# Half of the last weight's quarters prepared in layer 3 and parked as split parts, and raw operands loaded ahead of the weight blocks

## The chip, the cores and the metric

The kernel runs on one core of a Trainium2 chip. A core has five engines that work side by side, each through its own queue of instructions in a fixed order: TensorE (PE, matmuls), VectorE (DVE), ScalarE (ACT), GpSimd (POOL) and SyncE (SP, which here only issues DMAs). DMAs are also issued from POOL's queue and, a few, from ACT's. The metric is the device time of one execution in microseconds; lower is better.

## The reference, cut to what matters

```python
proj = einsum('bhsd,df->bhsf', x, w_phi)           # for q and for k
proj = proj - max(abs(proj), axis=-1, keepdims=True)
phi  = concatenate([exp(proj), exp(-proj)], axis=-1)
kv   = einsum('bhsf,bhsd->bhfd', phi(k), v);  z = sum(phi(k), axis=2)
attn = einsum('bhsf,bhfd->bhsd', phi(q), kv) / (phi(q) . z + 1e-6)
x = attn reshaped to (2304, 512)
h = maximum(maximum(x @ w1, x @ w2), x @ w3)        # 512 -> 768, layer 1
x = h @ w_out                                       # 768 -> 512, layer 2
h = x @ w_in                                        # 512 -> 2048, layer 3
g = maximum(h, 0) + alpha * minimum(h, 0)
out = g @ w_out2                                    # 2048 -> 512, the output blocks
```

4 batches, 8 heads, 576 positions, so 2304 tokens. The weights arrive as 64-bit floats; the results must be good to float32.

## The kernel before, in words

**Accuracy.** Every operand of a large product is kept as two tiles, `hi` (the value rounded to TensorE's format, a copy by ACT, L70) and `lo` (the rest, a subtraction by VectorE, L76). A product is three matmuls: hi x hi, hi x lo, lo x hi. A weight comes in as raw 64-bit words (tile `st`, 512 KB, loaded at L496 by SP) and is turned into 32-bit floats (tile `wt`) by one ACT instruction (L83) and four of VectorE (L85 to L91). What is then added or subtracted between such tiles goes through `both` (L517).

**Stages.** The 16 attention pairs run first, interleaved with layer 1 (TensorE line L270, matmuls `p<-x,w123t`). Each result `ho` of layer 1 goes to DRAM (`h_d`, POOL, L446). Layer 2 (L664, matmuls `p<-x,wo`) has 8 steps `c`; it leaves sums of token halves in DRAM (`y_d`). Layer 3 (L757) works by a Strassen-Winograd scheme of seven products instead of eight: 16 units, unit n being token group `tp` = n // 4 and quarter `q` = n % 4 of the columns. A unit has three PSUM tiles, `pb`, `pc` and `sums`; `sums` is added to in steps and copied out by ACT between them (`kept`, tile `s`, L766), and one more copy goes into `g` (L806). TensorE may go on into `sums` only when the copy is done. The result goes through `prelu` (ACT `neg`, L776; VectorE, L777) and by POOL to DRAM (`g_d`, L778).

**The output blocks** (L841, matmuls `acc<-wq,o`) are 9 blocks of 256 tokens. Each takes the 2048 inputs in two halves, and a half is 7 products of 12 matmuls, 84 in all. For a half, `left` loads raw data `a` from `g_d` (L705, two DMAs of 512 KB), forms sums `wt` of them (L718 to L731) and splits seven operands `o`. The weights `wq` are 28 granules (`needs`, L735): 7 combinations of each of four pieces p of `w_out2`; p = 0, 1 serve half 0, p = 2, 3 half 1. The combinations are formed early (`do_quarters`, L532) and parked in DRAM as plain floats (`q_d`, L530, POOL). `split_q` (L737) later reads each back (L742, SP) and splits it on ACT and VectorE into a tile of the pool `ring` or `ring2`. Part of half 0 of block 0 is done between the matmuls of the last two units of layer 3; for block 0 the weights of half 0 are split in layer 3's last units, those of half 1 around its end.

**Order.** The functions that prepare weights put their steps in one list `todo`, in the order of L589: the four pieces of `w_out2`, then `w_out`, then the four quads of `w_in`. `convert(n)` takes n steps from its front: two per unit of layer 1, three per step of layer 2 (L683), three per unit of layer 3 (L811, where the list is soon empty). `stage` (L493) keeps loads of `st` ahead of their use, three at first. Tiles of one tag rotate through a fixed number of buffers, so a load waits until the old tile's last reader is done, and a tile placed in a closed pool's memory waits for the old pool's last users (the second half's `a` and the `o` of the output blocks take over memory that layer 3 used). A scheduler in the framework, which goes by dependencies, a cost model and priorities, then writes each engine's order; on the chip each engine keeps to it.

Of the kernel before, what the change touches and what calls it, by code (L numbers as in the profile page):

```python
# [19 lines left out]
P = 128  # L20
# [33 lines left out]
def tile_kernel(ctx: ExitStack, tc: tile.TileContext, qT, kT, tails, v, w_phi, w1, w2, w3, w_out, w_in, w_out2, alpha, out):  # L54
# [54 lines left out]
    r_d = dram.tile([B, NPAIR, 2, S], F32, name="r_d")  # L109
    g_d = dram.tile([NF2, P, NTOK], F32, name="g_d")  # L110
    y_d = dram.tile([NT2, 7, P, 2 * CH], F32, name="y_d")
    q_d = dram.tile([4, 7, P, 512], F32, name="q_d")

    def bank(tag, bufs, nm):
        return ps.tile([P, 512], F32, tag=tag, bufs=bufs, name=nm)
# [370 lines left out]
    def granule(pool, nm):  # L486

        return pool.tile([P, 2, 512], F32R, tag="w", name=nm)

    sources, staged = [], []  # L490
    todo = []

    def stage():  # L493
        if sources:
            st = big(U32, [P, 1024], "st")
            nc.sync.dma_start(st, sources.pop(0).bitcast(U32))  # L496
            staged.append(st)

    def big(dtype, shape, nm):
        return sp.tile(shape, dtype, tag="st", bufs=3, name=nm)  # L500

    def word():
        return sp.tile([P, 512], F32, tag="wt", bufs=8, name="wt")

    def words():

        wt = word()
        run(from_f64(staged.pop(0), wt))
        stage()
        return wt  # L510

    def split(dst, src):
        hi_act(dst[:, 0], src)
        sub(V, dst[:, 1], src, dst[:, 0])

    def both(dst, x, y, op=ALU.subtract):
        V.tensor_tensor(dst, x, y, op=op)  # L517
        return dst
# [7 lines left out]
    def do_out():  # L526
        return [lambda k=k: split_out(k) for k in range(NF1)], [w_out[k] for k in range(NF1)]

    def park(p, i, x):
        nc.gpsimd.dma_start(q_d[p, i], x)  # L530

    def do_quarters(p):  # L532
        b = {}

        def get(q):
            b[q] = words()

        def one():
            get(0)
            b[4] = both(word(), b[1], b[0])  # L540
            park(p, 0, b[0])
            park(p, 4, b[4])

        def two():
            get(3)
            park(p, 2, b[3])
            b[5] = both(word(), b[3], b[4])
            park(p, 5, b[5])
            park(p, 6, both(b[1], b[3], b[1]))

        def three_():
            get(2)
            park(p, 1, b[2])
            park(p, 3, both(word(), b[5], b[2]))

        return [lambda: get(1), one, two, three_], [w_out2[p, q] for q in (1, 0, 3, 2)]

    def do_quad(q):
        x = {}
        wi[q] = {}  # L560

        def get(n):
            x[n] = words()

        def to(i, n):
            pool = ring2 if (q == 0 and i < 4) or (q == 3 and i > 0) else ring
            wi[q][i] = granule(pool, "wi")
            split(wi[q][i], x[n])

        def second():  # L570
            get("22")
            x["s1"] = both(word(), x["21"], x["22"], ALU.add)

        def third():
            get("11")
            x["s2"] = both(word(), x["s1"], x["11"])
            x["s3"] = both(x["21"], x["11"], x["21"])
            to(0, "11")

        def fourth():  # L580
            get("12")
            to(1, "12")
            x["s4"] = both(x["12"], x["12"], x["s2"])

        steps = [lambda: get("21"), second, third, fourth]
        steps += [lambda i=i, n=n: to(i, n) for i, n in zip(range(2, 7), ("s2", "s1", "s3", "22", "s4"))]
        return steps, [w_in[q, a, b] for a, b in ((1, 0), (1, 1), (0, 0), (0, 1))]

    for steps, src in [do_quarters(p) for p in range(4)] + [do_out()] + [do_quad(q) for q in range(4)]:  # L589
        todo += steps  # L590
        sources += src

# [19 lines left out]
    def convert(n):  # L612
        for _ in range(min(n, len(todo))):
            todo.pop(0)()
# [38 lines left out]
    for c in range(2 * B):  # L653
        p2 = [double(tag, "p2") for tag in SETS[c % 2]]
        if c == 0:
            p2.reverse()
        if c + 1 < 2 * B:
            for kk in range(NF1 // 2):
                load_h(c + 1, kk)
        for ms in ((0, 1), (2, 3)) if c == 0 else (range(KT),):  # L660
            for k, m in ((k, m) for k in range(NF1) for m in ms):
                cs = slice(m * P, (m + 1) * P)
                for n, (x, y) in enumerate(three(wo[k][:, 0, cs], wo[k][:, 1, cs], *hs[c, k])):
                    nc.tensor.matmul(p2[m // 2][1][:, m % 2], x, y, start=k + n == 0, stop=k == NF1 - 1 and n == 2)  # L664
        tp = c // 2
        for b in range(2):
            Y[b, c % 2] = yo = z_tile("yo")
            A.activation(yo, p2[b][1], AF.Copy)
            if c % 2 == 0:
                nc.scalar.dma_start(y_d[tp, b], flat(yo))  # L670
        if c % 2:
            nc.scalar.dma_start(y_d[tp, 6], flat(Y[1, 1]))
            t1, t2, t3 = (z_tile("yt") for _ in range(3))
            both(t1, Y[0, 1], Y[0, 0])
            both(t2, Y[1, 1], t1)
            both(t3, Y[1, 1], Y[0, 1])
            t4 = both(Y[1, 0], Y[1, 0], t2)
            for i, t in zip((2, 3, 4, 5), (t2, t1, t3, t4)):
                nc.gpsimd.dma_start(y_d[tp, i], flat(t))
        if c == 2 * B - 1:  # L680
            for i in range(6):
                load_y(0, i)
        convert(3)  # L683

    T = P
    ORDER = (0, 5, 6, 4, 1, 3, 2)
# [5 lines left out]
            return (None, ring2, ring2, ring2, ring2, ring, ring)[n]  # L692
        return None if half == 0 and n == 0 else op4

    def left(block, half):

        ready[block, half] = res = {}
        if half and block:
            a = up.tile([P, 2, 4, 2 * T], F32, tag="a", bufs=1, name="a")
            a = [a[:, kh] for kh in range(2)]  # L700
        else:
            a = [big(F32, [P, 4, 2 * T], "a") for _ in range(2)]
        for kh in range(2):
            r = slice(kh * 8 + half * 4, kh * 8 + half * 4 + 4)
            nc.sync.dma_start(a[kh], g_d[r, :, block * 2 * T : (block + 1) * 2 * T].rearrange("f p n -> p f n"))  # L705
        (a00, a10), (a01, a11) = ((x[:, :, :T], x[:, :, T:]) for x in a)
        s1, s2, s3, s4 = (word().rearrange("p (f n) -> p f n", f=4) for _ in range(4))

        def factor(i, src):
            home = factor_home(block, half, len(res))  # L710
            o = granule(home, "o") if home else big(F32R, [P, 2, 512], "o")
            ov = o.rearrange("p a (f n) -> p a f n", f=4)
            hi_act(ov[:, 0], src)
            sub(V, ov[:, 1], src, ov[:, 0])
            res[i] = o

        factor(0, a00)
        V.tensor_tensor(s1, a10, a11, op=ALU.add)  # L718
        V.tensor_tensor(s2, s1, a00, op=ALU.subtract)
        yield  # L720
        factor(5, s2)
        V.tensor_tensor(s3, a00, a10, op=ALU.subtract)
        yield
        factor(6, s3)
        yield
        factor(4, s1)
        yield
        factor(1, a01)
        yield
        factor(3, a11)  # L730
        V.tensor_tensor(s4, a01, s2, op=ALU.subtract)  # L731
        yield
        factor(2, s4)
# [3 lines left out]
    def split_q(count):  # L737
        for _ in range(count):
            n = len(wq)
            p, i = needs[n]  # L740
            wl = word()
            nc.sync.dma_start(wl, q_d[p, i])  # L742
            wq[p, i] = granule(ring if n < 16 or n >= 26 else ring2, "wq")
            split(wq[p, i], wl)

    load_y(0, 6)

# [40 lines left out]
    for n, (tp, q) in enumerate(units):  # L788
        sums, u1 = nxt
        if (tp, q) == (NT2 - 1, 0):  # L790
            convert(len(todo))
        g0, g1 = result(), result()
        _, pb = double("db", "pb")
        mults(pb, tp, q, 1, True)
        V.tensor_tensor(g0[:, :, 0], pb, u1, op=ALU.add)
        mults(sums, tp, q, 2, False)
        u2 = kept(sums)
        _, pc = double("dc", "pc")
        mults(pc, tp, q, 3, True)
        mults(sums, tp, q, 4, False)  # L800
        u3 = kept(sums)
        V.tensor_tensor(g1[:, :, 1], pc, u3, op=ALU.add)
        if n + 1 < len(units):
            nxt = begin(n + 1)
        mults(sums, tp, q, 5, False)
        A.activation(g1[:, :, 0], sums, AF.Copy)  # L806
        mults(pc, tp, q, 6, False)
        V.tensor_tensor(g0[:, :, 1], pc, u2, op=ALU.add)  # L808
        prelu(g1, tp, 4 * q + 2)
        prelu(g0, tp, 4 * q)  # L810
        convert(3)  # L811
        if tp == NT2 - 1:
            if q == 0:
                first = left(0, 0)
                run(first)
            split_q((2, 7, 7, 7)[q])
    zp_ctx.close()
    xp_ctx.close()
# [103 lines left out]
```

## Time and profile before

| | |
|---|---|
| median of 3 runs | 886.14 us (883.64 to 888.54) |
| profiled execution | 882.21 us, span 880.4 us |
| TensorE busy | 869.1 us (99%) |
| VectorE busy | 678.7 us (77%) |
| ACT busy | 490.8 us (56%) |
| POOL busy | 158.3 us (18%) |
| mean granted TensorE clock | 0.998 |

A row of a timeline reads: start, duration, engine, line, operation, out<-in, size, how many of the same in a row, and in brackets how long the engine had been idle and what ended that. Matmuls overlap in the pipeline, so the distance of starts, and not the duration of one, is their pace. The granted clock is a share of the full 2.4 GHz.

### The profile page before, as it was taken

Reading aid. Unit: us, or ns where it says so; the run is one execution under the profiler, and the core shown is the slowest. Engines: PE = TensorE matmul, PEld = TensorE weight load, DVE = VectorE, ACT = ScalarE, POOL = GpSimd, SP = SyncE. Lnnn points to the kernel's source line nnn. Section 1 sums busy time; section 2 is a strip of 40 time slices with the busy share of each in tenths; the row PEclk is TensorE's granted clock in tenths of the full one; section 3 lists DMA queues with packets and bytes.
Section 4 is the critical chain, followed back from the end, with each engine's and each line's share of the span. In section 5 each row is a group of like instructions: output and inputs, shape, how many; then the busy total and the mean of one; then the engine's idle time right before and its main releaser. Section 6 shows DMA issues by size and latency. Waiting matters only on the chain.

```text
span 880.4 us, 17440 instructions
## 1 busy us (share of the span) xinstructions
PE 869.1 (99%) x6631; PEld 856.2 (97%) x6631; DVE 678.7 (77%) x1290; ACT 490.8 (56%) x1017; POOL 158.3 (18%) x278
## 2 busy tenths in 40 slices
PE   9999999999999999999999999999999999999998
PEld 8888999999999999999999999999999999999998
DVE  5689878778887879889999454746488889977791
ACT  4677657677776752334365354646477654444440
POOL 0354213222232135331101001111111100000000
PEclk9999999999999999999999999999999999999999
DMA  6455553222332158886489644835358645544321
GB/s 233 140 159 168 169 180 91 77 79 89 85 90 76 29 176 286 291 276 191 159 284 304 203 147 146 271 131 194 111 183 267 214 152 173 165 123 140 120 73 48
DMA packets 70436, 142.99 MB, mean 162 GB/s; under 512 B 9152, under 2 KB 36176, under 8 KB 70352
## 3 DMA queue, kind: packets, MB, share of 16 engines
q1 hardware_dynamic: 53664, 92.95, 33.8%
q0 software_dynamic: 14816, 45.26, 15.0%
q10 hardware_dynamic: 1872, 3.67, 1.2%
q8 instruction: 52, 0.85, 0.4%
q14 instruction: 32, 0.26, 0.1%
HBM read 93.07 MB, written 46.34 MB: 158 GB/s over the span
## 4 chain that ended last, share of the span: by engine, by line
PE 85%; DVE 6%; DMA 4%; issue 2%; ACT 1%; POOL 1%; DVEq 0%; POOLq 0%; ACTq 0%; SPq 0%
PE acc L841 20%; PE p L270 17%; PE sums L757 11%; PE p L664 8%; PE pj L270 6%; PE pn L270 6%; PE pc L757 6%; PE kvp L298 3%; PE kvp L311 3%; PE pb L757 3%; PE pt L373 2%; DVE wt L89 1%; DVE wt L91 1%; DMA xr<-h_d 1%; DMA nd<-nd 1%
## 5 line engine op out<-in xcount | busy, mean ns | idle before, releaser
L270 PE MATMUL p<-x,w123t 128*128 128x288 f32 x1728 | 249.1, 298 | 0.9 <-DVE ho L444 0.9
L270 PEld LDWEIGHTS p<-x,w123t 128*128 128x128 f32 x1728 | 234.5, 188 | 2.2 <-DVE ho L444 1.1
L841 PE MATMUL acc<-wq,o 128*128 128x256 f32 x1512 | 182.3, 283 | 2.5 <-ACT o L70 2.2
L841 PEld LDWEIGHTS acc<-wq,o 128*128 128x128 f32 x1512 | 181.5, 190 | 2.9 <-ACT o L70 2.4
L757 PE MATMUL sums<-x,wi 128*128 128x288 f32 x768 | 107.7, 295 | 0.3 <-ACT s L766 0.3
L757 PEld LDWEIGHTS sums<-x,wi 128*128 128x128 f32 x768 | 103.9, 188 | 0.6 <-ACT s L766 0.6
L664 PE MATMUL p<-x,wo 128*128 128x288 f32 x576 | 77.1, 296 | 1.5 <-ACT x L70 0.8
L664 PEld LDWEIGHTS p<-x,wo 128*128 128x128 f32 x576 | 76.6, 188 | 1.9 <-ACT x L70 1.0
L70 ACT ACTIVATE o<-wt 128x512 fp32r<-128x512 f32 x72 | 44.4, 629 | 56.4 <-PE acc L841 28.6
L777 DVE SCALAR_TENSOR_TENSOR g<-neg,al,g 128x576 f32<-128x576 f32 x64 | 50.1, 811 | 23.7 <-ACT neg L776 23.7
L217 DVE TENSOR_REDUCE mx<-pj 128x4 f32<-128x512 f32 (+1 forms) x80 | 49.7, 629 | 18.4 <-PE pj L270 18.1
L766 ACT ACTIVATE s<-sums 128x576 f32<-128x576 f32 x48 | 31.1, 648 | 45.4 <-PE sums L757 44.1
L778 POOL DMA_DIRECT2D g_d<-g x32 | 22.9, 714 | 162.5 <-DVE g L777 160.2
L446 POOL DMA_DIRECT2D h_d<-ho x48 | 27.8, 579 | 120.5 <-DVE ho L444 102.6
L76 DVE TENSOR_TENSOR o<-wt,o 128x512 fp32r<-128x512 f32 x72 | 48.0, 681 | 1.7 <-ACT o L70 1.7
L83 ACT ACTIVATE wt<-st 128x512 f32<-128x512 f32 x38 | 25.3, 673 | 41.7 <-DMA st<-in_w_out 33.4
L250 ACT ACTIVATE ke<-pj,mx 128x128 f32<-128x128 f32 x96 | 36.5, 380 | 20.1 <-DVE mx L217 20.1
L70 ACT ACTIVATE o<-a 128x512 fp32r<-128x512 f32 x54 | 33.1, 626 | 19.8 <-PE acc L841 18.5
L776 ACT ACTIVATE neg<-g 128x576 f32<-128x576 f32 x64 | 40.1, 675 | 6.2 <-DVE g L808 5.9
L251 ACT ACTIVATE ke<-pj,my 128x128 f32<-128x128 f32 x96 | 37.0, 386 | 11.0 <-DVE my L248 10.8
L298 PEld LDWEIGHTS kvp<-v,ke 128*128 128x128 f32 x320 | 40.1, 191 | 2.1 <-ACT ke L243 0.3
L298 PE MATMUL kvp<-v,ke 128*128 128x128 f32 x320 | 41.8, 276 | 0.0
(155 smaller groups left out, 1699.5 us busy)
## 6 DMA issues: line engine op xcount, KB each, us to landing
g_d<-g POOLq DMA_DIRECT2D x32, 576.0 KB, 3.6
a<-g_d SPq DMA_DIRECT2D x36, 512.0 KB, 4.4
st<-in_w_out SPq DMA_DIRECT2D x22, 512.0 KB, 5.3
wst<-in_w SPq DMA_DIRECT2D x18, 512.0 KB, 4.8
st<-in_w_in SPq DMA_DIRECT2D x16, 512.0 KB, 3.8
yr<-y_d SPq DMA_DIRECT2D x28, 288.0 KB, 3.4
v<-in_v SPq DMA_DIRECT2D x16, 480.0 KB, 3.6
q_d<-wt POOLq DMA_DIRECT2D x28, 256.0 KB, 6.0
```

The costliest lines, as they stand in the source:

```text
L70: A.activation(dst, src, AF.Copy)
L76: eng.tensor_tensor(dst, src, hi.bitcast(F32), op=ALU.subtract)
L217: V.tensor_reduce(mx, pv, axis=AX.X, op=ALU.max, apply_absolute_value=True, negate=True)
L250: A.activation(ev[:, a, 0], pv[:, a], AF.Exp, bias=mx[:, a : a + 1])
L251: A.activation(ev[:, a, 1], pv[:, a], AF.Exp, bias=my[:, a : a + 1], scale=-1.0)
L270: nc.tensor.matmul(dst, x, y, start=i == 0, stop=i == len(ops) - 1, **kw)
L298: nc.tensor.matmul(kvp[:, j * P : (j + 1) * P], e[:, c], rv[:, t, j // 2 : j // 2 + 2].rearrange("p a d -> p (a d)"), start=first, stop=t ...
L664: nc.tensor.matmul(p2[m // 2][1][:, m % 2], x, y, start=k + n == 0, stop=k == NF1 - 1 and n == 2)
L757: nc.tensor.matmul(dst[:, j], a, b, start=start and n == 0, stop=n == len(ops) - 1, skip_group_check=True)
L776: A.activation(neg, gv[:, j], AF.Relu, scale=-1.0)
L777: V.scalar_tensor_tensor(gv[:, j], neg, al[:, f + j : f + j + 1], gv[:, j], op0=ALU.mult, op1=ALU.add)
L841: nc.tensor.matmul(acc[i], x, y, start=half == 0 and f == 0 and n == 0 and place[i][1] == 0, stop=half == 1 and f == 3 and n == 2, skip_gr ...
```

## The change

- The list of L589 is cut in two: pieces 0 and 1 of `w_out2`, `w_out` and the quads of `w_in` as before, and pieces 2 and 3 behind them all. For these two `do_quarters` gives 8 small steps instead of 4.
- Their results are not parked as plain floats: `park` splits them at once into a tile `qt` in the ring of `st` and writes hi and lo (512 KB) to a new DRAM tile `qs_d`. `split_q` then loads such a granule straight into `wq`, with no work for ACT and VectorE.
- The ring of `st` has 4 buffers instead of 3, and the space that POOL's DMA descriptors take is halved. `words` loads a next `st` only when fewer than `depth` are waiting: 3, and 2 from layer 3's first unit on.
- `convert` takes 1, 2, 2, 3, 3, 3, 3, 3 steps in the 8 steps of layer 2, and in layer 3 two per unit, none in unit 1.
- `left` is divided: `load_left` issues the loads of `a`, and it is called for half 1 of block 0 ahead of the loads of the weight granules.

```diff
-    q_d = dram.tile([4, 7, P, 512], F32, name="q_d")
+    q_d = dram.tile([2, 7, P, 512], F32, name="q_d")
+    qs_d = dram.tile([2, 7, P, 1024], F32, name="qs_d")
...
-    sources, staged = [], []
+    sources, staged, depth = [], [], [3]
...
-        return sp.tile(shape, dtype, tag="st", bufs=3, name=nm)
+        return sp.tile(shape, dtype, tag="st", bufs=4, name=nm)
...
         run(from_f64(staged.pop(0), wt))
-        stage()
+        if len(staged) < depth[0]:
+            stage()
...
     def park(p, i, x):
-        nc.gpsimd.dma_start(q_d[p, i], x)
+        if p < 2:
+            nc.gpsimd.dma_start(q_d[p, i], x)
+            return
+        t = big(F32R, [P, 2, 512], "qt")
+        split(t, x)
+        nc.gpsimd.dma_start(qs_d[p - 2, i], t.bitcast(F32).rearrange("p a n -> p (a n)"))
...
+        steps = [lambda: get(1), one, two, three_]
+        if p > 1:
+            steps = [
+                lambda: get(1),
+                lambda: (get(0), park(p, 0, b[0])),
+                lambda: park(p, 4, b.setdefault(4, both(word(), b[1], b[0]))),
...
+            ]
...
-    for steps, src in [do_quarters(p) for p in range(4)] + [do_out()] + [do_quad(q) for q in range(4)]:
+    order = [do_quarters(p) for p in range(2)] + [do_out()] + [do_quad(q) for q in range(4)]
+    for steps, src in order + [do_quarters(p) for p in range(2, 4)]:
...
-        convert(3)
+        convert((1, 2, 2, 3, 3, 3, 3, 3)[c])
...
+    def left(block, half):
+
+        ready[block, half] = res = {}
+        if (block, half) not in raw:
+            load_left(block, half)
+        a = raw[block, half]
...
+            wq[p, i] = t = granule(ring if n < 16 or n >= 26 else ring2, "wq")
+            if p > 1:
+                nc.sync.dma_start(t.bitcast(F32).rearrange("p a n -> p (a n)"), qs_d[p - 2, i])
+                continue
             wl = word()
             nc.sync.dma_start(wl, q_d[p, i])
-            wq[p, i] = granule(ring if n < 16 or n >= 26 else ring2, "wq")
-            split(wq[p, i], wl)
+            split(t, wl)
...
-        convert(3)
+        depth[0] = 2
+        convert(2 if n != 1 else 0)
         if tp == NT2 - 1:
             if q == 0:
                 first = left(0, 0)
                 run(first)
+                load_left(0, 1)
             split_q((2, 7, 7, 7)[q])
...
-    nc = bacc.Bacc("TRN2", target_bir_lowering=False, num_devices=1, dynamic_dma_scratch_size=8192)
+    nc = bacc.Bacc("TRN2", target_bir_lowering=False, num_devices=1, dynamic_dma_scratch_size=4096)
```

The change also moves what the scheduler writes. Lines of the changed kernel are some 30 higher there: L875 is the old L841, L789 the old L757, L798 the old L766, L808 the old L776, L838 the old L806, L747 to L760 the old L718 to L731.

First TensorE, around the end of layer 3: `acc` are the output block's matmuls, the others layer 3's last two units. Before:

```order
L757 MATMUL pb<-x,wi 128x288 x12
L757 MATMUL sums<-x,wi 128x288 x12
L841 MATMUL acc<-wq,o 128x256 x5
L757 MATMUL pc<-x,wi 128x288 x12
L841 MATMUL acc<-wq,o 128x256 x9
L757 MATMUL sums<-x,wi 128x288 x12
L841 MATMUL acc<-wq,o 128x256 x26
L757 MATMUL sums<-x,wi 128x288 x12
L841 MATMUL acc<-wq,o 128x256 x2
L757 MATMUL pc<-y,wi 128x288 x12
L841 MATMUL acc<-wq,o 128x256 x1470
```

The changed kernel, the same place:

```order
L789 MATMUL sums<-x,wi 128x288 x36
L875 MATMUL acc<-wq,o 128x256 x18
L789 MATMUL pc<-y,wi 128x288 x12
L789 MATMUL pb<-x,wi 128x288 x12
L789 MATMUL sums<-x,wi 128x288 x12
L875 MATMUL acc<-wq,o 128x256 x3
L789 MATMUL pc<-x,wi 128x288 x12
L875 MATMUL acc<-wq,o 128x256 x11
L789 MATMUL sums<-x,wi 128x288 x12
L875 MATMUL acc<-wq,o 128x256 x16
L789 MATMUL sums<-x,wi 128x288 x12
L875 MATMUL acc<-wq,o 128x256 x1464
```

42 of the 84 matmuls of half 0 stood before the end of layer 3, and now 48; the first run of them has moved up behind the `sums` of unit 14, whose PSUM tile it takes over.

Next VectorE, behind the seven operands of half 1 of block 0. `o_9225` (before) and `o_9226` (after) are the lo part of block 1's first operand, `a_9217`, `a_9218` and `a_9219` raw data of block 1's first half, `a_9351` and `a_9352` of its second. Before:

```order
L76 TENSOR_TENSOR o_9225<-a_9217,o_9225 128x512
L718 TENSOR_TENSOR wt_9221<-a_9217,a_9218 128x512
L719 TENSOR_TENSOR wt_9222<-wt_9221,a_9217 128x512
L722 TENSOR_TENSOR wt_9223<-a_9217 128x512
L731 TENSOR_TENSOR wt_9224<-a_9218,wt_9222 128x512
L718 TENSOR_TENSOR wt_9354<-a_9351 128x512
L76 TENSOR_TENSOR o_9230<-wt_9222,o_9230 128x512
```

The changed kernel, the same place:

```order
L747 TENSOR_TENSOR wt_9355<-a_9352 128x512
L76 TENSOR_TENSOR o_9231<-wt_9223,o_9231 128x512
L76 TENSOR_TENSOR o_9235<-wt_9224,o_9235 128x512
L76 TENSOR_TENSOR o_9238<-wt_9222,o_9238 128x512
L748 TENSOR_TENSOR wt_9356<-wt_9355,a_9352 128x512
L751 TENSOR_TENSOR wt_9357<-a_9352 128x512
L76 TENSOR_TENSOR o_9241<-a_9219,o_9241 128x512
L76 TENSOR_TENSOR o_9244<-a_9219,o_9244 128x512
L76 TENSOR_TENSOR o_9248<-wt_9225,o_9248 128x512
L76 TENSOR_TENSOR o_9226<-a_9218,o_9226 128x512
```

The first sum over `a_9352` has moved ahead of all operands of block 1, and the operand that block 1 starts with has moved to the end of them. In both kernels SP issues the two loads of this half's raw data behind the last load for `wq`, and only when the last write of `g_d` has landed.

Last ACT, in units 0 and 1 of layer 3 of the changed kernel; `st_7823` is a raw quarter, `s_7054` the first kept sums within unit 1, and `qt` are the split tiles on their way to `qs_d`:

```order
L838 ACTIVATE g_6908<-sums_6892 128x2x288
L808 ACTIVATE neg_7006<-g_6908 128x576
L808 ACTIVATE neg_7009<-g_6908 128x576
L70 ACTIVATE qt_7833<-wt_7825 128x512
L83 ACTIVATE wt_7992<-st_7823 128x512
L808 ACTIVATE neg_7013<-g_6907 128x576
L808 ACTIVATE neg_7016<-g_6907 128x576
L70 ACTIVATE qt_7988<-wt_7986 128x512
L798 ACTIVATE s_7054<-sums_6965 128x576
```

Before, there were only `s`, `g` and `neg` in this place; the conversion and the splits have moved in from layer 1.

## Rows read from the trace of the kernel before

**Rows 1.** The page, busy time of each engine, share of the span, instructions.

```profile
PE 869.1 (99%) x6631; PEld 856.2 (97%) x6631; DVE 678.7 (77%) x1290; ACT 490.8 (56%) x1017; POOL 158.3 (18%) x278
```

**Rows 2.** Waits of TensorE: total us, times, longest us.

```profile
PE acc L841 <- ACT o L70: 2.2, 1, 2.2
...
PE p L270 <- DVE ho L444: 0.9, 1, 0.9
PE p L664 <- ACT x L70: 0.8, 1, 0.8
PE p L664 <- DVE x L76: 0.7, 1, 0.7
...
PE acc L841 <- DVE o L76: 0.3, 1, 0.3
```

**Rows 3.** Timeline of TensorE, the end of layer 3.

```profile
696.02 0.40 PE L841 MATMUL acc<-wq,o 128*128 128x256 f32 x2
...
697.85 5.16 PE L841 MATMUL acc<-wq,o 128*128 128x256 f32 x42
```

**Rows 4.** The chain of waits, 697 to 725: start, us, what.

```profile
700.89 3.00 DMA wt<-q_d
...
705.33 0.61 DVE o L76
...
705.98 19.12 PE acc L841 x146
```

**Rows 5.** Table by stretch: busy us (instructions) by engine, clock, DMA share, GB/s.

```profile
704.00:706.00 2.00, 0.52 (x3) 0.32 (x3) 1.49 (x4) 2.00 (x4) 0.00 (x0) 1.00 1.02 415
706.00:708.00 2.00, 2.00 (x12) 2.00 (x13) 2.00 (x4) 2.00 (x5) 0.00 (x0) 0.66 0.06 21
708.00:710.00 2.00, 2.00 (x11) 2.00 (x11) 1.90 (x4) 0.88 (x2) 0.00 (x0) 0.50 0.87 245
710.00:712.00 2.00, 2.00 (x19) 2.00 (x18) 0.33 (x1) 0.00 (x0) 0.00 (x0) 0.98 1.09 366
```

**Rows 6.** The chain of waits before layer 2's first matmuls.

```profile
433.27 3.63 DMA st<-in_w_in
```

**Rows 7.** Timeline of ACT, unit 0 of layer 3.

```profile
519.18 0.65 ACT L766 ACTIVATE s<-sums 128x576 f32<-128x576 f32 x1 [1.94 <-PE sums L757]
```

**Rows 8.** The page, DMA issues: KB each, median us to landing.

```profile
g_d<-g POOLq DMA_DIRECT2D x32, 576.0 KB, 3.6
...
st<-in_w_out SPq DMA_DIRECT2D x22, 512.0 KB, 5.3
...
q_d<-wt POOLq DMA_DIRECT2D x28, 256.0 KB, 6.0
```

**Rows 9.** The page, costliest groups: busy us, mean ns, idle before.

```profile
L766 ACT ACTIVATE s<-sums 128x576 f32<-128x576 f32 x48 | 31.1, 648 | 45.4 <-PE sums L757 44.1
```

**Rows 10.** The chain of waits, unit 1 of layer 3.

```profile
528.72 1.60 PE sums L757 x12
...
531.92 4.80 PE sums L757 x36
```

**Rows 11.** Timeline of POOL, the last write of layer 3.

```profile
703.22 0.72 POOL L778 DMA_DIRECT2D g_d<-g  x1 [1.95 <-DVE g L777]
```

**Rows 12.** Timeline of VectorE around the end of layer 3.

```profile
700.18 1.29 DVE L76 TENSOR_TENSOR wq<-wt,wq 128x512 fp32r<-128x512 f32 x2
701.38 1.54 DVE L777 SCALAR_TENSOR_TENSOR g<-neg,al,g 128x576 f32<-128x576 f32 x2
...
705.85 1.89 DVE L76 TENSOR_TENSOR o<-wt,o 128x512 fp32r<-128x512 f32 x3
```

**Rows 13.** Timeline of ACT at the end of layer 3.

```profile
696.22 0.65 ACT L806 ACTIVATE g<-sums 128x576 f32<-128x576 f32 x1 [1.43 <-PE sums L757]
```

**Rows 14.** The tiles `a` from 700 to 720: min/median/max of one, first and last start.

```profile
L705 SPq DMA_DIRECT2D a<-g_d x4: 359/411/501, 706.9 to 716.2; - x4
...
DMA to landing us min/median/max: 4.3/5.2/6.2
```

More of the change, by code (lines that the diff above doesn't have):

```diff
@@ L554, in three_ @@
             park(p, 3, both(word(), b[5], b[2]))
-        return [lambda: get(1), one, two, three_], [w_out2[p, q] for q in (1, 0, 3, 2)]
+        steps = [lambda: get(1), one, two, three_]
[4 more added lines that the diff above has]
+                lambda: park(p, 4, b.setdefault(4, both(word(), b[1], b[0]))),
+                lambda: (get(3), park(p, 2, b[3])),
+                lambda: park(p, 5, b.setdefault(5, both(word(), b[3], b[4]))),
+                lambda: park(p, 6, both(b[1], b[3], b[1])),
+                lambda: (get(2), park(p, 1, b[2])),
+                lambda: park(p, 3, both(word(), b[5], b[2])),
+            ]
+        return steps, [w_out2[p, q] for q in (1, 0, 3, 2)]
     def do_quad(q):
@@ L693, in factor_home, with load_left @@
         return None if half == 0 and n == 0 else op4
-    def left(block, half):
-        ready[block, half] = res = {}
+    raw = {}
+    def load_left(block, half):
         if half and block:
@@ L705, in left @@
             nc.sync.dma_start(a[kh], g_d[r, :, block * 2 * T : (block + 1) * 2 * T].rearrange("f p n -> p f n"))
+        raw[block, half] = a
+    def left(block, half):
[3 more added lines that the diff above has]
+        a = raw[block, half]
         (a00, a10), (a01, a11) = ((x[:, :, :T], x[:, :, T:]) for x in a)
```

## The prediction

> **What bounds the kernel now.** I read the page first: TensorE is busy 869.1 of the 880.4 us [rows 1], so the change can win only where TensorE waits, loses clock, or waits anew. The list of TensorE's waits comes next [rows 2]; the reader should see how little is in it: 0.9 us in layer 1 (on VectorE's `ho`), 0.8 and 0.7 us at the start of layer 2 (on the operands `x`), and 2.2 and 0.3 us at the first operand `o` of the last weight's second half. That last place, the handover from layer 3 to the output blocks, is where a wait costs twice. TensorE's timeline [rows 3] and the chain of waits [rows 4] date it: layer 3 ends at 697.85 us, 42 matmuls of half 0 follow, and then TensorE stands until 705.98, because the chain runs through a read of a parked quarter (3.00 us from 700.89), its split, and only then the split of `o` on VectorE, 0.61 us at 705.33. The table of stretches [rows 5] shows the second price: after that gap the granted clock is 0.66, then 0.50 (the lower of the two levels, 1.2 of 2.4 GHz), then 0.98. Lost: 2 x 0.34 + 2 x 0.50 + 2 x 0.02 = 1.72 us. The 146 matmuls from 705.98 take 19.12 us, so one takes (19.12 - 1.72) / 146 = 0.119 us and a half of a block (84) 10.0. Block 1 starts in before at 705.98 + 82 x 0.119 + 1.72 = 717.5 us (two of half 1 ran ahead).
>
> **The change part by part.** The profiled execution took 882.21 us, span 880.4; the median is 886.14, so 3.9 above. I sum against the profiled one and add the difference to the median.
>
> *Less conversion in layers 1 and 2.* Half of the 28 parked pieces leave layer 1. The 0.9 us wait there is behind VectorE, whose last work before `ho` is conversion; I take -0.7 (0 to -0.9). At the start of layer 2 the chain shows a weight load (3.63 us from 433.27) and then conversions ahead of the `x` that TensorE wants [rows 6]. The weight of layer 3 now arrives earlier, and layer 2 starts with one step instead of three: -1.5 (0 to -1.5). What is late next in both places: nothing that the waits show.
>
> *The quarters in layer 3.* Their arithmetic is the same, but ACT's queue in the first units now holds `wt<-st` (L83), and the third block of rows of the order shows it ahead of two `neg` and of the kept sums `s_7054`. The load `st_7823` it wants goes into a buffer of the `st` ring that the parked `qt_7688` must leave first. In before, unit 0's copy of its second sums ends at 519.8 [rows 7]; the hi and lo parts of `qt_7688` follow it (two times about 0.65), so POOL issues its write near 521.5. No row has a 512 KB write of this kind; the nearest are 3.6 us (576 KB, same queue) and 6.0 (256 KB of `q_d`) [rows 8]. The load after it lies between 3.63 [rows 6] and 5.3 us [rows 8]. With 3.6 and 4.5 the load lands at 529.7, and five ACT instructions of about 0.65 us [rows 9] (L83, two `neg`, one `qt`, `s_7054` itself) end at 532.9. TensorE needs `s_7054` at 531.92, where it goes on into `sums` [rows 10]: +1.0. With the long ends it is 533.0 and 536.2: +4.2. With both short ends 3.6 and 3.63: nothing. I take the middle because the DMA rows nearest in size are the shorter write. The first kept sums of layer 3 also find one more 0.62 us copy ahead of them: +0.6. Together +1.6 (0 to +4.8). The smaller descriptor space for POOL's queue has no row; its issue takes 0.72 us now [rows 11], and I give it 0, at most +0.5.
>
> *Parked split.* Fourteen ACT and fourteen VectorE splits leave the handover, fourteen reads of 512 KB instead of 256 replace them. So the first `o` of half 1 no longer queues behind `wq`: in before, L777 ends at 702.92 with two `wq` subtractions ahead of it (1.29 us) [rows 12]. That was 5.1 us after layer 3's end; less 1.29, and less a part of the copies of `wq` on ACT that held up `neg`, I take 3.5 (3.8 without that part). The last write of `g_d` follows 0.3 later, at 3.8.
>
> *More of half 0 ahead.* 48 instead of 42 of its 84 matmuls now stand before the end of layer 3, so layer 3 ends 6 x 0.119 = 0.71 later. The first run of 18 stands right behind `sums` of unit 14 and writes the bank that ACT's L838 still reads: that copy starts 0.20 after the sums end and takes 0.65 [rows 3, 13], so TensorE waits 0.85 there, hidden by nothing. Layer 3 ends at 697.85 + 0.71 + 0.85 = 699.4. The last 36 of half 0 take 4.3: half 1 can start at 703.7, and its first `o` (lo) is done at 699.4 + 3.5 + 0.68 = 703.6. The 2.5 us of waiting and its clock go.
>
> *The raw operands of block 1.* This is the step that I think decides. In before VectorE does the first operand of block 1 (`o_9225`) before any sum over new data. Now `wt_9355`, the first sum over block 1's second half, stands ahead of `o_9226` and of six more operands, and VectorE takes its instructions in order. Its data, `a_9352`, are two reads which may only start when the last write of `g_d` has landed, since they take memory of that tile. In before that write issues at 703.22 [rows 11] and the reads start at 706.9 [rows 14], 3.7 later. Now the write issues at 699.4 + 3.8 = 703.2, the same, since the later end of layer 3 eats what VectorE gains. Reads of this kind take 4.3 to 6.2 us to land, median 5.2, and one holds SP's queue for 0.4 [rows 14], so the second issues 0.4 after the first: both are there near 712.5. Reads of `wq` now run beside the write until 703.7, where there were smaller ones; at 415 GB/s [rows 5] the 512 KB of one cost at most 1.3 us, of two 2.5, so I add 0.5 (0 to +2.5): 713.0. From there `o_9226` is nine instructions at 0.605 (three in 1.89 us, the last 0.68 [rows 12]) and its own 0.68 away: 713.0 + 5.45 + 0.68 = 719.1. Half 1 ends at 703.7 + 10.0 = 713.7; three matmuls of block 1 can run, then TensorE waits 5 us on VectorE, double the gap of before. Start of block 1, less the three: 719.1 - 0.36 = 718.7 against 717.5, +1.3. And the clock, which the gap of before took down, falls after this one too: +1.7 (0 to +2.5). Handover: +3.0 (0 to +6).
>
> The Trainium skill, "DMA: Bandwidth & Descriptors", section on queues, rings and completion order, says that each DMA engine switches between the queues it has work for, a packet at a time. By that rule the write of `g_d` would share with the waiting reads of `wq` and move at half rate, 1.4 us longer, and the whole would come to 889.4 rather than the forecast; the rows have no such pair, so none of the sum rests on it.
>
> Sum: -0.7 - 1.5 + 1.6 + 3.0 = +2.4, so 886.14 + 2.4 = 888.5 us.
>
> **The rivals.**
> A, the handover is not a loss: the reads land in the least time, 4.3, and no `wq` is in their way, so `o_9226` is done at 706.9 + 0.4 + 4.3 + 6.1 = 717.7, a wait of some 3.6 us, which the clock forgives, as it did the shorter waits of rows 2. Handover 0, layer 3 costs nothing either: -0.7 - 1.5 = -2.2, 883.9. For it: the splits do leave the handover. Against it: the shorter gap of 2.5 us at the same place did bring the clock down.
>
> B, slower: ACT, blocked by `wt<-st` in units 0 and 1 behind the write of `qt` (6.0) and a long load (5.3), +4.8 instead of +1.6. Total -2.2 + 4.8 + 3.0 = +5.6, 891.7. It decides once write and load together take over 10.3 us after 521.5 (TensorE's slack in unit 1 is used up at 7.2; the long ends make 11.3). For it: `q_d` writes did take 6.0 by the median. Against it: the DMA share is lower in layer 3 than where those were written.
>
> C, transfers share: `a_9352` lands 2.0 later than I take it, 890.5. For it: the reads of `wq` double in size just there. Against it: they are paced by TensorE's releases, some 1.4 us apart, and the last starts at 703.7.
>
> D, the change does not do what it says in layers 1 and 2: the waits there stay, as VectorE is still the busier engine, and the rest is as forecast: +4.6, 890.7.
>
> **How the numbers follow.** Forecast 0.50 (its own range 886 to 891), A 0.15, B 0.15, C 0.12, D 0.08. A measurement tells no change below 0.5%, 4.4 us, so faster means under 881.7 and slower over 890.6. Faster: a fifth of A, some of the forecast's lower edge and waits that I don't see: 0.07. Slower: 0.10 of the forecast, two thirds of B (0.10), half of C and D (0.10): 0.30. The same 0.63. The range reaches from below A to above B, each by about what the runs of before differ: 882.5 to 893.5.
>
> **What would show it.** Right: one wait of TensorE at the output line on VectorE's `o` of 4 to 6.6 us near 714 to 719, with granted clock near 0.5 to 0.7 in the two to four us behind it, and VectorE's L747 waiting on the DMA `a<-g_d`; no wait at the start of half 1 at 703.7; a wait of 0.8 us on ACT's L838 near 682; the two waits on `x` in layer 2's start gone; ACT's L83 waiting on `st` in the first units of layer 3. Wrong: block 1 without a wait (then A), more than 2 us of TensorE's waits on `s` in layer 3 (B), `a<-g_d` landing after 714 (C), or a wait on `x` at layer 2's start as long as before (D).

## The result, and the profile after

The changed kernel takes 896.57 us, the median of 6 runs (893.26 to 897.99), beside 884.52 (882.93 to 888.54) for the kernel before: ratio 1.0128, 95% interval 1.0099 to 1.0156. It is slower by some 11 us. The forecast was 888.5, 2.4 above the 886.14 that it started from, and its range ended at 893.5. The profiled execution took 895.86 us, span 894.1, so the two profiled spans differ by 13.7 us.

First, the list of TensorE's waits in the changed kernel (us in total, times, longest us), which answers to [rows 2]:

```profile
PE acc L875 <- DVE o L76: 9.9, 1, 9.9
PE sums L789 <- ACT s L798: 2.6, 2, 1.6
PE p L684 <- ACT x L70: 1.7, 1, 1.7
...
PE acc L875 <- ACT g L838: 0.7, 1, 0.7
PE p L684 <- DVE x L76: 0.3, 1, 0.3
```

The wait on `ho` of layer 1 and the 2.2 us on `o` at the start of half 1 are gone. In their place stands one wait of 9.9 us. The timeline of TensorE (start us, busy us, instructions, idle time before them) says where, and answers to [rows 3]:

```profile
687.08 2.40 PE L875 MATMUL acc<-wq,o 128*128 128x256 f32 x18 [0.74 <-ACT g L838]
...
704.00 15.09 PE L875 MATMUL acc<-wq,o 128*128 128x256 f32 x123
728.96 11.26 PE L875 MATMUL acc<-wq,o 128*128 128x256 f32 x74 [9.87 <-DVE o L76]
```

Layer 3 ends at 704.00, and 123 matmuls follow without a gap: the last 36 of half 0, the 84 of half 1 and three of block 1. Then TensorE stands for 9.87 us. The chain of waits names what it stands for; its rows answer to [rows 4]:

```profile
708.40 8.48 DMA g_d<-g
...
717.07 0.37 SPq L726
717.44 0.05 issue
717.49 5.22 DMA a<-g_d
...
722.79 0.69 DVE wt L747
723.48 1.81 DVE o L76 x3
725.29 0.60 DVE wt L748
725.89 0.60 DVE wt L751
726.49 1.33 DVE o L76 x3
727.82 0.39 issue
728.22 0.70 DVE o L76
```

Read it from the end. `o` at 728.22 is the lo part of `o_9226`, the first operand of block 1. Ahead of it in VectorE's queue stand the nine instructions that begin with L747, and L747 waits for `a_9352`, whose read waits for the last write of `g_d`. That write, issued at 708.40, takes 8.48 us; the last one in before took 3.7 ([rows 11], [rows 14]). The operand itself needed none of it: on ACT's timeline the hi part of `o_9226`, which has the same input, is done at 714.2:

```profile
713.59 0.61 ACT L70 ACTIVATE o<-a 128x512 fp32r<-128x512 f32 x1
```

The table by stretch (us; busy us and instructions of TensorE, its weight loads, VectorE, ACT and POOL; granted clock; DMA share; GB/s) has the price behind the wait, and answers to [rows 5]:

```profile
724.00:726.00 2.00, 0.00 (x0) 0.00 (x0) 2.00 (x5) 0.00 (x0) 0.00 (x0) 0.50 0.00 0
...
728.00:730.00 2.00, 1.04 (x5) 1.05 (x6) 2.00 (x4) 1.61 (x4) 0.00 (x0) 0.50 0.49 105
730.00:732.00 2.00, 2.00 (x11) 2.00 (x11) 2.00 (x5) 0.72 (x2) 0.00 (x0) 0.50 0.48 165
732.00:734.00 2.00, 2.00 (x12) 2.00 (x12) 2.00 (x5) 0.00 (x0) 0.00 (x0) 0.54 0.63 161
```

The granted clock is at its lower level from the idle time on until near 734: 1.04 x 0.50 + 2 x 0.50 + 2 x 0.46 = 2.4 us lost, against 1.7 in before.

Why the write is slow shows in the DMA share, last but one of the columns, over the 24 us around layer 3's end. Before:

```profile
692.00:704.00 12.00, 11.01 (x90) 10.80 (x89) 10.07 (x16) 7.68 (x15) 1.43 (x2) 1.00 0.64 191
704.00:716.00 12.00, 10.52 (x74) 10.32 (x75) 7.60 (x13) 5.33 (x10) 0.00 (x0) 0.86 0.59 203
```

After:

```profile
692.00:704.00 12.00, 12.00 (x97) 12.00 (x95) 5.47 (x8) 3.82 (x7) 0.72 (x1) 1.00 0.97 352
704.00:716.00 12.00, 12.00 (x103) 12.00 (x102) 7.97 (x12) 9.22 (x17) 1.43 (x2) 1.00 1.01 398
```

VectorE falls from 10.07 to 5.47 us in the first stretch: the splits have gone, as meant. The transfers rise from 191 to 352 GB/s and fill all 16 DMA engines. Bytes have taken the place of arithmetic, at a place where the DMA engines had a third free and needed more than that.

The rest of the 13.7 us, by the same timelines: up to layer 2's first matmul nothing (435.17 before, 435.11 after); layer 2 +1.9, with the starts of layer 3 at 513.61 and 515.48; layer 3 +4.3, to 697.85 and 704.00; from there to the end +7.5 (182.55 and 190.10).

### The profile page after: what moved, and what is told of

Its sections match the earlier page's. It is cut to its first block, busy times and chain, and to the rows that moved or that the text cites. A ratio compares the mean times of both kernels' runs of the same rounds, so it can differ in the third digit from the quotient of the medians.

```text
span 894.1 us, 17383 instructions
## 1 busy us (share of the span) xinstructions
PE 872.3 (98%) x6631; PEld 858.5 (96%) x6631; DVE 680.9 (76%) x1290; ACT 490.2 (55%) x1017; POOL 161.4 (18%) x278
## 4 chain that ended last, share of the span: by engine, by line
PE 76%; DMA 10%; DVE 5%; issue 4%; POOL 2%; ACT 2%; SPq 0%; DVEq 0%; POOLq 0%; ACTq 0%
PE acc L875 18%; PE p L271 17%; PE sums L789 11%; PE p L684 7%; PE pc L789 5%; PE pj L271 4%; PE pn L271 4%; PE kvp L312 3%; PE pb L789 3%; DMA r_d<-dc 2%; DMA xr<-r_d 1%; PE pt L374 1%; PE kvp L299 1%; DMA g_d<-g 1%; DMA dc<-nd 1%
## 5 line engine op out<-in xcount | busy, mean ns | idle before, releaser
L875 PE MATMUL acc<-wq,o 128*128 128x256 f32 x1512 | 183.1, 284 | 10.7 <-DVE o L76 9.9
L875 PEld LDWEIGHTS acc<-wq,o 128*128 128x128 f32 x1512 | 182.2, 191 | 11.3 <-DVE o L76 10.1
L789 PE MATMUL sums<-x,wi 128*128 128x288 f32 x768 | 108.0, 295 | 2.6 <-ACT s L798 2.6
L789 PEld LDWEIGHTS sums<-x,wi 128*128 128x128 f32 x768 | 104.0, 188 | 3.1 <-ACT s L798 3.1
L798 ACT ACTIVATE s<-sums 128x576 f32<-128x576 f32 x48 | 31.0, 648 | 44.3 <-PE sums L789 42.1
L447 POOL DMA_DIRECT2D h_d<-ho x48 | 30.1, 627 | 132.8 <-DVE ho L445 111.3
L808 ACT ACTIVATE neg<-g 128x576 f32<-128x576 f32 x64 | 40.2, 676 | 8.8 <-DVE g L840 8.5
L442 ACT ACTIVATE s<-p 128x288 f32<-128x288 f32 x48 | 20.3, 424 | 38.9 <-PE p L271 36.6
```

What stands on the lines that cost most here:

```text
L789: nc.tensor.matmul(dst[:, j], a, b, start=start and n == 0, stop=n == len(ops) - 1, skip_group_check=True)
L808: A.activation(neg, gv[:, j], AF.Relu, scale=-1.0)
L875: nc.tensor.matmul(acc[i], x, y, start=half == 0 and f == 0 and n == 0 and place[i][1] == 0, stop=half == 1 and f == 3 and n == 2, skip_gr ...
```

## The experiments

Each was timed against the kernel before on the same chip. The theory: block 1 starts late because `o_9226` stands behind L747 in VectorE's queue, and L747 behind a transfer that it doesn't need. The rival: the DMA engines are full, so block 1 is late in whatever order VectorE works. A second question is why the write takes 8.48 us: the 512 KB reads of the parked split quarters, or the loads of raw data that were put ahead of them.

| kernel | us (range, runs) | ratio to before, 95% |
|---|---|---|
| changed kernel | 896.57 (893.26–897.99, 6) | 1.0128, 1.0099–1.0156 |
| e1, operand first | 885.44 (881.46–887.70, 10) | 1.0013, 0.9997–1.0030 |
| e2, half the bytes of the reads | 891.03 (889.32–892.19, 4) | 1.0081, 1.0062–1.0100 |
| e3, parked unsplit | 888.32 (885.71–890.42, 7) | 1.0045, 1.0028–1.0062 |
| e4, no early loads | 895.64 (894.99–896.72, 4) | 1.0136, 1.0120–1.0152 |
| e5, e1 + layer 2's loads first | 881.14 (880.00–885.47, 12) | 0.9972, 0.9956–0.9987 |
| e6, e1 + last quarters held | 891.72 (887.26–891.87, 6) | 1.0075, 1.0052–1.0098 |
| e7, e5 + last quarters held | 888.09 (887.76–888.71, 6) | 1.0047, 1.0028–1.0065 |
| e8, e7 held to unit 1 only | 883.95 (881.16–887.79, 12) | 0.9998, 0.9981–1.0014 |
| e9, e8 with five held | 883.23 (881.81–886.84, 12) | 1.0002, 0.9987–1.0016 |
| e10, e5 + parked unsplit | 890.89 (890.14–892.41, 6) | 1.0083, 1.0068–1.0098 |

**e1: the operand first.** One column of `o_9226`'s lo part is copied into the place that the sum overwrites, so the sum can no longer be put ahead of it. No transfer changes.

```diff
+        if (block, half) == (1, 1):
+            V.tensor_copy(s1[:, 0, :1], ready[1, 0][0][:, 1, :1].bitcast(F32))
         V.tensor_tensor(s1, a10, a11, op=ALU.add)
```

> One copy of a single column makes VectorE's first sum over block 1's second half wait for the last operand of block 1's first half; loads, splits and bytes stay as in the changed kernel. Theory (the sum stood ahead of the operand in VectorE's queue, and its late data held up block 1): the wait of 9.9 us at block 1 goes, no wait takes its place at half 1 of block 1 since the raw data land some 6 us before they are needed there, and the clock stays up: -9.9 -2.4, about 884.4 us. Rival (the full DMA queues are the cause, and the order only decides where the wait shows): the wait comes back 10 us later at half 1 of block 1, 893 us or more.

Measured: level with the kernel before, and 11.1 us less than the changed kernel by the medians (10.2 by the ratios). Its waits:

```profile
PE p L684 <- ACT x L70: 2.9, 1, 2.9
PE sums L791 <- ACT s L800: 2.1, 2, 1.6
...
PE acc L877 <- ACT g L840: 0.7, 1, 0.7
PE acc L877 <- DMA wq<-qs_d: 0.5, 2, 0.3
```

The wait on `o` is gone altogether, while the stretches of this kernel are as full as before it (DMA share and GB/s last):

```profile
692.00:704.00 12.00, 12.00 (x96) 12.00 (x95) 6.22 (x9) 2.57 (x4) 0.83 (x2) 1.00 0.98 334
704.00:716.00 12.00, 12.00 (x102) 12.00 (x101) 10.17 (x16) 10.58 (x19) 1.43 (x2) 1.00 1.02 402
```

The last write of `g_d` is issued at 710.18, and the reads behind it start at 718.90, 8.7 later. So at block 1 the slow write alone costs nothing; it costs where the queue of an engine hangs on it. What the full engines still cost in this kernel are the 0.5 us on `wq<-qs_d`. The theory holds, and the rival falls.

**e2: half the bytes.** Of the split quarters only the hi half is read; POOL fills the lo half with zeros, so the product is that of the hi parts.

```diff
-                nc.sync.dma_start(t.bitcast(F32).rearrange("p a n -> p (a n)"), qs_d[p - 2, i])
+                nc.sync.dma_start(t[:, 0].bitcast(F32), qs_d[p - 2, i, :, :512])
+                nc.gpsimd.memset(t[:, 1].bitcast(F32), 0.0)
```

> Each read of a parked split granule brings only its hi half, 256 KB instead of 512, and the lo half is set to zero by GpSimd: so the lo parts of half 1's weights are left out of the product. The order on VectorE is that of the changed kernel. Theory (the write of g_d waits 8.5 us behind the doubled reads): it lands in about 3.7 us again, the wait at block 1 falls from 9.9 to about 5 us, the clock still falls behind it; 891.3 us. Rival (the order alone sets the wait): 896.6 us as before.

Measured: 5.5 us less than the changed kernel. The chain, and then the same two stretches:

```profile
706.66 4.99 DMA g_d<-g
...
712.26 5.07 DMA a<-g_d
...
723.57 6.53 PE acc L876 x39
```

```profile
692.00:704.00 12.00, 12.00 (x97) 12.00 (x97) 5.94 (x10) 3.41 (x6) 4.97 (x10) 1.00 0.71 246
704.00:716.00 12.00, 12.00 (x104) 12.00 (x103) 6.25 (x10) 8.51 (x17) 2.95 (x5) 1.00 0.74 256
```

With the DMA share down to 0.71 and 0.74 the write takes 4.99 us instead of 8.48; the read behind it stays (5.07 and 5.22). So the bytes of these reads slow the write, though the 3.7 us that were expected did not come back. Block 1 starts at 723.57, 5.4 earlier, with 5.7 us of waits left (2.26 and 3.48); 1.7 of the 5.4 come from layer 3, which ends at 702.26 in this execution.

**e3: parked unsplit.** The quarters go out and come back as floats of 256 KB and are split after the read, as in before; all else as changed.

```diff
-        if p < 2:
-            nc.gpsimd.dma_start(q_d[p, i], x)
-            return
-        t = big(F32R, [P, 2, 512], "qt")
-        split(t, x)
-        nc.gpsimd.dma_start(qs_d[p - 2, i], t.bitcast(F32).rearrange("p a n -> p (a n)"))
+        nc.gpsimd.dma_start(q_d[p, i], x)
...
-            if p > 1:
-                nc.sync.dma_start(t.bitcast(F32).rearrange("p a n -> p (a n)"), qs_d[p - 2, i])
-                continue
```

> All of the change but the split parking: pieces 2 and 3 are prepared in layer 3, parked as plain floats (256 KB) and split after their read. VectorE's order at block 1 is as in the changed kernel. Theory: the write of g_d lands in about 3.7 us, the wait at block 1 is 4 to 5 us, the wait for the first operand of half 1 comes back with up to 2.5 us as the splits are in the handover again, layer 3's start costs less than 2.5 us; about 891 us. Rival (parking split is worth its bytes, since the splits in the handover cost more than the reads): 897 us or more.

Measured: 8.3 us less than the changed kernel. The last write is issued at 707.70, and the reads start at 711.42, 3.7 later, as in before. Together with e2 this shows that the write is slow when more is moved beside it: 8.48, 4.99 and 3.7 us with reads of 512, 256 and 256 KB, at 398 GB/s, 256 and 222 moved from 704 to 716. Why e2 and e3 differ at the same size is not isolated; in e2 the last of these reads is issued 0.1 us behind the write, in e3 2.3 us ahead of it. The halved space for POOL's descriptors, which the change brought too, is the same in e2 and e3, so it alone does not make the 8.48. The expectation for the whole was 891 and thus high, since the wait moved: it now stands at half 1 (timeline of TensorE),

```profile
709.71 0.50 PE L866 MATMUL acc<-wq,o 128*128 128x256 f32 x2 [2.23 <-ACT o L70]
712.32 17.93 PE L866 MATMUL acc<-wq,o 128*128 128x256 f32 x136 [2.11 <-DVE o L76]
```

behind the splits. So half 1 starts only at 712.32 and runs until some 724, an estimate from 82 matmuls of 0.119 us and some 1.6 us of lower clock. By then the data of L747 (here L741) are long there: VectorE waits 1.00 us for them and starts the sum at 716.88. Block 1 starts without a wait.

**e4: no early loads.**

```diff
-                load_left(0, 1)
```

> The raw operands of block 0's second half are loaded where before they were, not ahead of the weight granules; all else is the changed kernel, and VectorE's order at block 1 is the same. Theory (loading ahead is not what moved the order): within 1.5 us of the changed kernel, 895 to 898 us. Rival (the loads put ahead push the later ones back): the wait at block 1 shrinks to 5 us or less, 891 us.

Measured: as the changed kernel, with one wait of 9.5 us on `o` at the same line. That the raw data of half 1 are loaded ahead of the weight granules is no part of the cause.

**e5: layer 2's operands first.** On top of e1 the loads of the last eight raw quarters are held back until layer 2's first two chunks of `h` have been asked for.

```diff
-        if sources:
+        if sources and not (hold and len(sources) <= 8):
             st = big(U32, [P, 1024], "st")
+            if 5 < len(sources) <= 8:
+                V.tensor_copy(st[:, :1].bitcast(F32), hs[1, 4][1][:, :1].bitcast(F32))
...
+        while hold or (c == 0 and len(staged) < depth[0]):
+            hold.clear()
+            stage()
```

> On top of e1_dve_first: the first three loads of the late quarters wait, by a copy of one column, for layer 2's second set of operands, so on SyncE the loads of these operands (hr) stand ahead of them. Theory (layer 2's start waits for hr, which queued behind two 512 KB loads): the wait of 2 to 3 us on x and the fall of the clock behind it go, at most the 1.5 us of before stay; 885.4 - 2.9 = 882.5 us. Rival (VectorE is what layer 2's start waits for, as it was before): no change, 885 us.

Measured: 881.14 us, below the kernel before by 0.28% (0.13% to 0.44%), and 4.3 us below e1. What the edit moved is on SP's queue at the start of layer 2. In the changed kernel:

```profile
415.34 21.50 SPq L497 DMA_DIRECT2D st<-in_w_in  x5
437.47 0.93 SPq L497 DMA_DIRECT2D st<-in_w_out  x2
438.45 9.18 SPq L626 DMA_DIRECT2D hr<-h_d  x5
```

In e5:

```profile
417.08 21.39 SPq L499 DMA_DIRECT2D st<-in_w_in  x5
438.52 12.46 SPq L628 DMA_DIRECT2D hr<-h_d  x8
451.07 0.89 SPq L499 DMA_DIRECT2D st<-in_w_out  x2
```

The loads of `hr`, from which layer 2's operands `x` are made, start no earlier than in the changed kernel, though layer 2 itself begins 1.6 us later in e5. But in the changed kernel two loads of 512 KB stand right ahead of them, and the first `hr` takes 7.29 us (chain, from 438.45), the seven from 430 to 450 take 5.5 in the median; in e5 the median is 3.4, and TensorE runs from layer 1 into layer 2 without a gap:

```profile
436.75 15.54 PE L689 MATMUL p<-x,wo 128*128 128x288 f32 x116
```

Beside e1 the gain stands by itself: layer 2 begins within 0.4 us of e1's (436.33 and 436.75) and lasts 76.4 us instead of 81.2.

**e6 and e7: the last quarters held back in layer 3.** The waits on `s` at the start of layer 3 were laid to ACT's conversion. So the last six quarters were held until their unit of layer 3 had begun, in e6 on e1 and in e7 on e5.

```diff
+            if len(sources) <= 6:
+                G.tensor_copy(st[:, :1].bitcast(F32), mark[0][:, 0, :1])
...
         sums, u1 = nxt
+        mark[0] = u1
```

> On top of e1_dve_first: the last six of the eight late quarters are loaded only once a unit of layer 3 that the program puts their conversion into has begun (a copy of one column from its kept sums), so their work no longer runs ahead into the start of layer 3. Theory (that work in front of yt and s on VectorE and ACT costs layer 3's start 2.1 us of waits): the waits on s go to 0.3 us or less; 885.4 - 2 = 883.4 us. Rival (the start waits for something else, or the held-back work blocks later units): 885 us or more.

> e5_hr_first and e6_gate together. Theory (three separate waits, each with its own cause): both gains add up, 885.4 - 2.9 - 2 = 880.5 us, below the kernel before by 3 us. Rival (the gains are one and the same, or what is saved is lost at the handover, where the queues are full): 882.5 us or more.

Measured: both slower, by 6.3 us against e1 and 7.0 against e5: the expectation failed. The wait on `s` fell to 0.3 us, and another came (waits of e7, then the chain in it):

```profile
PE pc L798 <- DVE g L844: 7.0, 3, 4.2
```

```profile
604.80 10.90 DMA a<-g_d
```

For the longest of the three waits, 4.2 us, it is the mechanism of block 1 a second time. In e7 VectorE's L756, again a sum of raw data, waits 5.63 us for that read, and the `g` behind it, which frees `pc`, comes late. The other two, 1.6 and 1.3 us, were not followed.

**e8 and e9: a shorter hold.** The six quarters (five in e9) are held to unit 1 only, and four steps a unit follow.

```diff
+        if n >= 1 and mark[0] is None:
+            mark[0] = u1
...
-        convert(2 if n != 1 else 0)
+        convert(2 if n < 1 else 4)
```

> As e7_both, but the held-back loads are let go all at once by unit 1's first sums, and four steps of conversion instead of two stand in each unit from unit 1 on, so the work is over before the raw operands of the output blocks are loaded. Theory (the 7 us of waits in e7_both came from late conversion meeting those loads on VectorE's queue; the start of layer 3 itself was cured): waits on pc gone, waits on s at most 1 us: 881.1 - 1.5 = 879.6 us. Rival (ACT and VectorE have no room in the first units for it, whatever its order): 882 us or more, with waits on s or pc in units 1 to 5.

> As e8_gate_early, but only the last five quarters are held back, so that one more is converted within layer 2. Theory as for e8_gate_early: 880 us, within 1 us of it. Rival: 882 us or more.

Measured: neither is better than e5, and neither can be told from the kernel before. The 879.6 and 880 us that the theory gave did not come; both times lie in the rival's range. In e8 the wait on `pc` is 4.0 us, in e9 that on `s` 2.3. How the start of layer 3 can be had without its 1.8 us (e5) stays open.

**e10: e5, parked unsplit.** Is parking split worth its bytes once VectorE's order is mended?

> e5_hr_first with plain parking in place of split parking (256 KB per piece, split on ACT and VectorE after the read). Theory (with VectorE's order mended, split parking is worth its bytes: it takes the splits out of the handover): the first operand of half 1 waits some 4 us again, and the clock falls behind it; 881.1 + 4 = 885 us. Rival (the parking makes no difference once the order is mended): 881 us.

Measured: 9.8 us slower than e5, where 4 were expected. The splits bring back half 1's waits,

```profile
PE sums L787 <- ACT s L796: 4.8, 1, 4.8
...
PE acc L873 <- DVE o L76: 2.2, 1, 2.2
PE acc L873 <- ACT o L70: 2.1, 1, 2.1
```

at the price of 4.3 us. The 4.8 on `s` were not expected: ACT's copy of the sums waits 4.64 us for a write of `y_d` (3.66 us in the chain), ahead of which the chain has POOL's write of a parked quarter. So with VectorE's order mended parking split saves the 4.3 us at half 1 and the clock behind them; what else of the 9.8 us comes from it no run tells apart. With the order left as it was, e3 had it the other way: unsplit was 8.3 us faster.

## Why the prediction was wrong, step by step

At the handover the place, the instructions and their order were right; a size was not. The step that failed is the raw operands of block 1, and in it the term "3.7 later" for the last write of `g_d`, with "so I add 0.5 (0 to +2.5)" for the reads of `wq` beside it: the write took 8.48 us. The profiled executions differ by 13.7 us and the forecast had 2.4. Of the 11.3 between them some 6 lie at the handover (9.0 instead of 3.0, with the 1.4 by which layer 3 ends later for it), 3.4 at the start of layer 2, where the mechanism was missed too, 1.2 in the rest of layer 3 and 0.6 in layer 1.

- *Layer 1* (-0.7): -0.1. The wait on `ho` went, and layer 2 began at the same time.
- *Start of layer 2* (-1.5): +1.9. "What is late next: nothing that the waits show" was wrong. The wait grew from 1.5 to 2.0 us behind `hr`, and one wait of 1.7 us took the clock down, where the two of before (0.8 and 0.7) had left it at 1.00: 0.78, 0.50 and 0.87 in the stretches from 446 to 452, 1.7 us lost. I had asked which conversions stand ahead of `x` on the engines, and not which loads stand ahead of `hr` on SP. What such a start costs shows in e5 beside e1, where the wait was 2.9 us: 4.3 us. The stretch with the lowest clock in the changed kernel:

```profile
448.00:450.00 2.00, 2.00 (x10) 2.00 (x10) 2.00 (x4) 2.00 (x5) 0.00 (x0) 0.50 0.84 231
```

- *Layer 3* (+1.6): the waits on `s` went from 0.3 to 2.6 us, so the size was near, but the place was another. Both are in unit 0. In the first, 1.63 us, ACT's copy is held by VectorE's `yt`; the second, 0.98, has ACT's L83 ahead of the unit's last kept sums, waiting 2.22 us for its load `st` (row below). That is what was argued for unit 1, one unit earlier; at `s_7054` itself TensorE did not wait. The whole of layer 3 took 4.3 more: 2.3 of this, 0.7 for six more matmuls, 0.74 on L838 and some 0.5 in small gaps.

```profile
526.82 0.66 ACT L83 ACTIVATE wt<-st 128x512 f32<-128x512 f32 x1 [2.22 <-DMA st<-in_w_out]
```

- *Half 0* (0.85 on L838, and 0.71 for the matmuls): 0.74 and 0.7. Right, as was half 1 without a wait.
- *The raw operands of block 1*. From the end of layer 3 the parts are, predicted and measured: issue of the last write 3.8 and 4.4; its landing 3.7 and 8.5; the reads 5.6 and 5.8, to which 0.5 was added; VectorE's instructions to the end of `o_9226` 6.1 and 6.1. All but one are within 0.6 us, and the one is off by 4.8. So the wait was 9.9 instead of 5, and the clock behind it cost 2.4 instead of 1.7.

Rival C named the cause, transfers that share, but priced it at 2.0 us. Its bound was the bytes of two reads at full rate, and its argument against was that the reads are paced by TensorE's releases, some 1.4 us apart. They were: SP issued 13 of them from 691.10 to 708.49, 1.45 us apart in the mean, most of them behind a release by TensorE, the last 0.1 us after the write's issue. But 512 KB every 1.45 us is 362 GB/s for these reads alone, so the DMA share was at 1 long before the write began, and the reads themselves landed late. From 690 to 730 (KB each, median us to landing), before and after:

```profile
wt<-q_d SPq DMA_DIRECT2D x5, 256.0 KB, 2.8
```

```profile
wq<-qs_d SPq DMA_DIRECT2D x13, 512.0 KB, 7.0
```

So the reads didn't only double in size there; there are 13 where there were five. The numbers at hand could have warned of it: 512 KB each 1.4 us is 374 GB/s, beside the 415 of [rows 5], in stretches that already had a DMA share near 0.6. The rule of the Trainium skill that was weighed ("DMA: Bandwidth & Descriptors", Queues, rings and completion order: each DMA engine goes from queue to queue by the packet) agrees with the trace in direction; by it the write would have been 1.4 us longer, and 4.8 was measured. Whether the turns between queues make the 8.5 us, or packets already on their way, no run here tells apart.

Rivals A and D do not fit: the handover cost 9.0 us, and of the waits in layers 1 and 2 only the second stayed, behind loads and not behind VectorE. B's waits in layer 3 (over 2 us on `s`) came, but in unit 0 and without deciding the result: e1 keeps 2.1 us of them and is level with before.

Taken together: the changed kernel loses some 11 us where one VectorE instruction stands nine places too early behind a transfer that the full DMA engines make late (e1 mends the order; e2 and e3 ease the transfer), and some 4 at the start of layer 2 (e5 against e1). With both mended it is 0.28% below the kernel before. Whether that kernel would gain from the second edit too wasn't tried.

## What to carry to other kernels

Where an engine works in order, look for the instruction whose data comes last and for what stands behind it: a slow transfer costs nothing until an operand that is wanted now is queued behind its first user, and one column copied as a dependency mends that. Work that is traded for bytes must be priced against the DMA share of the stretch that the bytes land in: near a share of 1 a landing time from a quieter stretch may not hold (the write here took 3.7 and 8.48 us). A steady pace of transfers is no safety; multiply it out. And of an urgent load ask which big loads stand just ahead of it on its queue; moving them behind it was worth 4 us here.

## What was not expected of the hardware

- The same write of 576 KB landed after 3.7 us at a DMA share of 0.59 (before) and 0.64 (e3) from 704 to 716, 4.99 at 0.74 (e2), 8.48 at 1.01 (changed) and 8.7 at 1.02 (e1). The read of 512 KB issued behind it took 5.22, as in before (median 5.2), though the share from 720 to 722 was 1.09.
- At the start of layer 2 one wait of 1.70 us and a further 0.27 lowered the granted clock to 0.50 for some 3 us; waits of 0.78 and 0.69 at the same place in before, with one matmul between them, did not lower it. The clock falls while TensorE still stands: 0.50 at 724 to 728, where it did nothing.
